# The first expert product by seven half-size products, on one core

## The chip, the cores and the metric

The kernel runs on one core of a Trainium2 chip. The metric is the time of one execution on the device, in microseconds (us); the median of three runs of the kernel before is 1385.63 us (1385.61 to 1385.86).

## The reference

Three stages follow one another on 1536 tokens (2 batches of 768) of width 512.

```
# 1: attention, 8 heads of 64; a key is kept if it is a sink (pos < n_sink) or 0 <= rel < window
a = softmax(where(keep, scale * q @ k.T, -1e9));  x = a @ v          # x: 1536 x 512
# 2: h = x @ w_in (512 x 1024); s = h * softmax(h); x2 = layernorm(s) * g_ln @ w_out (1024 x 512)
# 3: 8 experts, a gate from the logits of x2
P = exp(x2 @ w_gate - max)
for _ in range(8):
    P /= P.sum(1, keepdims=True) + 1e-09; P /= P.sum(0, keepdims=True) + 1e-09; P *= N / E
for e in range(E):
    out += P[:, e:e + 1] * (np.maximum(x2 @ w1[e], 0.0) @ w2[e])     # w1: 512 x 1024, w2: 1024 x 512
```

## The kernel before

All matrices are fp32. A product is made of three fast ones: each operand is split into a rounded part `hi` and a rest `lo`, and `mm3` adds hi x hi, hi x lo and lo x hi in PSUM. Such a step is therefore three matmul instructions (lines 80, 82 and 84). The rest comes from a subtraction: on VectorE for what leaves PSUM (`split_psum`: ScalarE copies, VectorE subtracts), on GpSimd for weights, which lie in SBUF (`split_sbuf`: a copy at line 73, subtractions of 512 columns at line 77).

Stages 1 and 2 go through 12 blocks of 128 tokens, one head at a time, in numbered slots. `h_unit` makes h for one block and starts its chain of softmax and LayerNorm steps: maximum (line 243), exponential on ScalarE, product, square on ScalarE, some small operations on `st` of which one is on GpSimd (line 260), scale and shift (line 264), the gains on GpSimd (line 265), and transposes on TensorE back to `lt`. `x2_unit` then multiplies two blocks with w_out in matmuls of 256 tokens; its PSUM tile `x2p` has one buffer, and `split_psum` takes it to `x2T`, with the tokens as columns.

Stage 3 is `experts`. For each expert e and each of 3 groups g of 512 tokens it computes the first product in 8 blocks of 128 of f, each with 4 blocks `kk` of d (12 matmuls of 512 columns), a relu on ScalarE and its rest on VectorE (tile `ht`), and then the second product for 4 blocks of tokens, 8 blocks of f each (24 matmuls of 512 columns). Results are added to `acc` on VectorE with the gate as a factor (line 690). Weights come in pieces of 512 KB; `pump` splits the next one when a piece has been used. The gate's logits and its iterations (`sinkhorn`) are cut into steps that `step_side` puts between the experts' matmuls.

Two things set the order. The program is written in slots, and `beside` gives attention work a higher priority than the matmuls that `bulk` takes from a queue. A scheduler then puts the instructions of each engine in a row, by priorities and by when it thinks that operands are ready; in that way matmuls of a later step come ahead where an earlier one waits. Pools that are opened and closed (`att`, `wp`, the PSUM pools) give their memory to what comes next, and what takes it waits for the last reader.

Of the kernel before, what the change touches and what calls it, by code (L numbers as in the profile page):

```python
# [21 lines left out]
def tile_sink_attention__then__solu_moe__then__sinkhorn_moe(  # L22
# [29 lines left out]
    W = 2 * C  # L52
    scale = 1.0 / float(D) ** 0.5
    PS = bass.MemoryType.PSUM

    def f32(ap):
        return ap.bitcast(F32)
# [33 lines left out]
    gains = const.tile([P, F], F32, name="gains")  # L91
# [43 lines left out]
    wraw = wpool = None  # L135
    w_extra = []
    w_tiles = [None] * 16
    w_count = [0]

    def w_slot():  # L140
        n = w_count[0] % (8 + len(w_extra))
        w_count[0] += 1
        tp, nm = (w_extra[n], f"we{n}") if n < len(w_extra) else (wpool, f"w{n - len(w_extra)}")
        return tp.tile([P, 2, F], F32R, name=nm, tag=nm)

    def w_split(src):
        raw = wraw.tile([P, F], F32, name="wr", tag="wr")
        nc.sync.dma_start(out=raw.rearrange("p (a b) -> p a b", b=src.shape[-1]), in_=src)
        t = w_slot()
        split_sbuf(t[:, 0], t[:, 1], raw)  # L150
        return t
# [75 lines left out]
    def h_unit(t, xt, pp, later, tr_q):  # L227
# [35 lines left out]
        def s_ln():  # L263
            nc.vector.tensor_scalar(u, u, nmu, c, ALU.add, ALU.mult)
            nc.gpsimd.tensor_tensor(u, u, gains, ALU.mult)
# [26 lines left out]
    x2T = {}  # L292

    def x2_unit(p, pp):

        lt = ln.pop(p)
        dst = x2T[p // 2]
        cs = slice((p % 2) * 2 * P, (p % 2 + 1) * 2 * P)
        for d2 in range(KD // 2):
# [9 lines left out]
            split_psum(dst[:, 0, ds, cs], dst[:, 1, ds, cs], ps)  # L309
# [238 lines left out]
    def logits_units(lp, ps_pool, lg):  # L548
# [7 lines left out]
        for g in range(NG):  # L556
            ps = ps_pool.tile([32, 512], F32, name="lgp", tag="mm")
            for kk in range(KD):
                nc.tensor.matmul(ps, lhsT=wg_r[:, kk], rhs=x2T[g][:, 0, kk], start=(kk == 0), stop=False)
            for kk in range(KD):  # L560
                nc.tensor.matmul(
                    ps[0:E], lhsT=wg_r[:, kk, 0:E], rhs=x2T[g][:, 1, kk], start=False, stop=(kk == KD - 1)
                )
            nc.scalar.activation(out=lt[:, g * 512:(g + 1) * 512], in_=ps[0:16], func=ACTF.Copy)
        yield
# [7 lines left out]
    def sinkhorn(lp, ps_pool, pr):  # L573

        lg = lp.tile([P, T, E], F32, name="lg")
        yield from logits_units(lp, ps_pool, lg)
# [34 lines left out]
    def experts(hpool, opool, lp, ps_pool):  # L611
        pr = lp.tile([P, T, E], F32, name="pr")
        acc = [opool.tile([P, DM], F32, name=f"acc{t}") for t in range(T)]
        side = sinkhorn(lp, ps_pool, pr)
        gate_done = [False]
        raw_blocks = []

        def step_side():
            if gate_done[0]:
                return  # L620
            try:
                next(side)
            except StopIteration:
                gate_done[0] = True
                for t in raw_blocks:
                    nc.gpsimd.tensor_scalar(acc[t], acc[t], pr[:, t, 0:1], 0.0, ALU.mult, ALU.add)

        w_list = []
        for e in range(E):
            for c in range(4):  # L630
                w_list.append(w1[e, :, c * 256:(c + 1) * 256].rearrange("(a p) f -> p a f", p=P))
            for c in range(4):
                w_list.append(w2[e, c * 256:(c + 1) * 256, :].rearrange("(a p) d -> p a d", p=P))
        NW = 8 + len(w_extra)
        got = {}
        done = [0]
        asked = [0]

        def pump():
            while asked[0] < len(w_list) and asked[0] < done[0] + NW:  # L640
                got[asked[0]] = w_split(w_list[asked[0]])
                asked[0] += 1

        pump()
        for e in range(E):
            for g in range(NG):
                hts = []
                for f in range(KF):
                    wt = got[8 * e + f // 2]
                    ps = ps_pool.tile([P, 512], F32, name="p1", tag="mm")  # L650
                    for kk in range(KD):
                        c0 = kk * 256 + f % 2 * P
                        for _ in mm3(
                            ps, wt[:, 0, c0:c0 + P], wt[:, 1, c0:c0 + P], x2T[g][:, 0, kk], x2T[g][:, 1, kk],
                            kk == 0, kk == KD - 1,
                        ):
                            yield 0.217
                    ht = hpool.tile([P, 2, 512], F32R, name="ht", tag="ht")
                    nc.scalar.activation(out=ht[:, 0], in_=ps, func=ACTF.Relu)  # L659
                    nc.vector.scalar_tensor_tensor(  # L660
                        out=ht[:, 1], in0=ps, scalar=0.0, in1=f32(ht[:, 0]), op0=ALU.max, op1=ALU.subtract
                    )
                    hts.append(ht)
                    if g == NG - 1 and f % 2:
                        done[0] += 1
                        pump()
                    if f % 2:
                        step_side()
# [349 lines left out]
```

## Time and profile before

| | |
|---|---|
| median of 3 runs | 1385.63 us |
| profiled execution, its own time | 1384.35 us |
| span of its trace | 1382.6 us |
| busy share of TensorE, VectorE, ScalarE, GpSimd | 98%, 30%, 21%, 25% |
| DMA queue, share of the 16 engines' span | 13.4% |

The span is that of the recorded instructions; the execution's own time is 1.75 us longer. Records of TensorE's matmuls overlap, since they are pipelined; distances between starts give their pace. Attention and x2 take the first 331 us of the span, the experts the rest.

### The profile page before, as it was taken

Reading aid. Unit: us, or ns where it says so; the run is one execution under the profiler, and the core shown is the slowest. Engines: PE = TensorE matmul, PEld = TensorE weight load, DVE = VectorE, ACT = ScalarE, POOL = GpSimd, SP = SyncE. Lnnn points to the kernel's source line nnn. Section 1 sums busy time; section 2 is a strip of 40 time slices with the busy share of each in tenths; the row PEclk is TensorE's granted clock in tenths of the full one; section 3 lists DMA queues with packets and bytes.
Section 4 is the critical chain, followed back from the end, with each engine's and each line's share of the span. In section 5 each row is a group of like instructions: output and inputs, shape, how many; then the busy total and the mean of one; then the engine's idle time right before and its main releaser. Section 6 shows DMA issues by size and latency. Waiting matters only on the chain.

```text
span 1382.6 us, 15901 instructions
## 1 busy us (share of the span) xinstructions
PE 1354.8 (98%) x6599; PEld 1125.9 (81%) x6599; DVE 411.9 (30%) x860; ACT 296.6 (21%) x628; POOL 348.1 (25%) x360
## 2 busy tenths in 40 slices
PE   7799999999999999999999999999999999999998
PEld 5688888887888888888888888888888888888886
DVE  7976544542233111221112221122211221112211
ACT  5765545522111100111001110011100110011100
POOL 7862111237005400440142025004400440042000
PEclk9979999999999999999999999999999999999999
DMA  7411211013001200110021012001200210010000
GB/s 215 144 39 32 46 32 24 24 38 100 16 1 48 74 0 1 62 61 0 6 65 52 0 31 76 16 1 46 77 0 0 62 61 0 0 62 24 23 31 33
DMA packets 68354, 56.24 MB, mean 41 GB/s; under 512 B 39984, under 2 KB 56368, under 8 KB 68272
## 3 DMA queue, kind: packets, MB, share of 16 engines
q1 hardware_dynamic: 68272, 55.13, 13.4%
q8 instruction: 54, 0.88, 0.3%
q14 instruction: 28, 0.23, 0.1%
HBM read 51.97 MB, written 3.15 MB: 40 GB/s over the span
## 4 chain that ended last, share of the span: by engine, by line
PE 92%; DVE 3%; ACT 1%; issue 0%; POOL 0%
PE p L80 25%; PE p L84 25%; PE p L82 25%; PE av L518 2%; PE x2p L80 2%; PE x2p L82 2%; PE x2p L84 2%; PE hp L84 1%; PE hp L80 1%; PE hp L82 1%; PE trp L490 1%; PE trp L320 1%; PE sc L80 1%; PE trp L276 1%; PE sc L82 1%; PE sc L84 0%
## 5 line engine op out<-in xcount | busy, mean ns | idle before, releaser
L659 ACT ACTIVATE ht<-p 128x512 fp32r<-128x512 f32 x192 | 114.8, 598 | 844.2 <-PE p L84 844.2
L80 PE MATMUL p<-x2T,w 128*128 128x512 f32 x672 | 262.0, 390 | 0.0
L82 PE MATMUL p<-x2T,w 128*128 128x512 f32 x672 | 261.5, 389 | 0.0
L84 PE MATMUL p<-x2T,w 128*128 128x512 f32 x672 | 261.5, 389 | 0.0
L80 PE MATMUL p<-w,ht 128*128 128x512 f32 x672 | 259.4, 390 | 0.0
L82 PE MATMUL p<-w,ht 128*128 128x512 f32 x672 | 258.9, 389 | 0.0
L84 PE MATMUL p<-w,ht 128*128 128x512 f32 x672 | 258.9, 389 | 0.0
L660 DVE SCALAR_TENSOR_TENSOR ht<-p,ht 128x512 fp32r<-128x512 f32 x192 | 132.7, 691 | 414.9 <-ACT ht L659 414.9
L73 POOL TENSOR_SCALAR w<-wr 128x1024 fp32r<-128x1024 f32 x56 | 59.1, 1056 | 610.3 <-PE p L84 601.9
L690 DVE SCALAR_TENSOR_TENSOR acc<-p,pr,acc 128x512 f32<-128x512 f32 x84 | 63.1, 751 | 382.4 <-PE p L84 382.4
L80 PEld LDWEIGHTS p<-x2T,w 128*128 128x128 f32 x672 | 126.2, 188 | 26.3
L84 PEld LDWEIGHTS p<-w,ht 128*128 128x128 f32 x672 | 126.2, 188 | 26.2
L84 PEld LDWEIGHTS p<-x2T,w 128*128 128x128 f32 x672 | 126.2, 188 | 26.2
L82 PEld LDWEIGHTS p<-x2T,w 128*128 128x128 f32 x672 | 126.2, 188 | 26.0
L80 PEld LDWEIGHTS p<-w,ht 128*128 128x128 f32 x672 | 126.2, 188 | 26.0
L82 PEld LDWEIGHTS p<-w,ht 128*128 128x128 f32 x672 | 126.2, 188 | 26.0
L77 POOL TENSOR_TENSOR w<-wr,w 128x512 fp32r<-128x512 f32 x112 | 142.1, 1290 | 4.3
L80 PE MATMUL x2p<-lt,w 128*128 128x256 f32 x192 | 56.1, 292 | 0.2
L82 PE MATMUL x2p<-lt,w 128*128 128x256 f32 x192 | 55.8, 290 | 0.0
L84 PE MATMUL x2p<-lt,w 128*128 128x256 f32 x192 | 54.6, 284 | 0.0
L518 PE MATMUL av<-v,at 128*128 128x64 f32 x352 | 52.8, 295 | 0.6 <-ACT at L493 0.5
L518 PEld LDWEIGHTS av<-v,at 128*128 128x128 f32 x352 | 49.9, 215 | 3.6 <-ACT at L493 1.4
(173 smaller groups left out, 1506.9 us busy)
## 6 DMA issues: line engine op xcount, KB each, us to landing
wr<-in_moe_w_dram SPq DMA_DIRECT2D x64, 512.0 KB, 3.3
raw<-in_moe_w_in_dram SPq DMA_DIRECT2D x8, 512.0 KB, 5.7
raw<-in_moe_w_out_dram SPq DMA_DIRECT2D x8, 512.0 KB, 3.6
qk<-in_q_dram SPq DMA_DIRECT2D x12, 256.0 KB, 2.8
qk<-in_k_dram SPq DMA_DIRECT2D x12, 256.0 KB, 2.9
v<-in_v_dram SPq DMA_DIRECT2D x12, 256.0 KB, 2.8
out_dram<-acc SPq DMA_DIRECT2D x12, 256.0 KB, 2.0
gains<-in_moe_g_ln_dram SPq DMA_DIRECT2D x1, 512.0 KB, 5.4
```

The source lines that it names most:

```text
L73: nc.gpsimd.tensor_scalar(hi, src, 1.0, 0.0, ALU.mult, ALU.add)
L77: nc.gpsimd.tensor_tensor(lo[:, cs], src[:, cs], f32(hi[:, cs]), ALU.subtract)
L80: nc.tensor.matmul(ps, lhsT=lh, rhs=rh, start=start, stop=False)
L82: nc.tensor.matmul(ps, lhsT=lh, rhs=rl, start=False, stop=False)
L84: nc.tensor.matmul(ps, lhsT=ll, rhs=rh, start=False, stop=stop)
L276: nc.tensor.transpose(ps[:, j], u[:, f * P:(f + 1) * P], ident)
L320: nc.tensor.transpose(ps[:, j], src[:, 2 * j:2 * j + 2].rearrange("p h d -> p (h d)"), ident)
L490: nc.tensor.transpose(ps[:, hh, z], a[:, o:o + P], ident)
L518: nc.tensor.matmul(self.av_ps[:, h], lhsT=at[:, hh, z], rhs=self.raw["v", tv][:, h], start=h == 0 and n == 0, stop=h == H - 1 and n == len ...
L659: nc.scalar.activation(out=ht[:, 0], in_=ps, func=ACTF.Relu)
L660: nc.vector.scalar_tensor_tensor(out=ht[:, 1], in0=ps, scalar=0.0, in1=f32(ht[:, 0]), op0=ALU.max, op1=ALU.subtract)
L690: nc.vector.scalar_tensor_tensor(out=acc[t], in0=ps, scalar=pr[:, t, e:e + 1], in1=acc[t], op0=ALU.mult, op1=ALU.add)
```

## The change

The first product is done by Strassen's scheme in the variant with 15 sums (Winograd's). The half sizes are of f (1024 to 2 x 512), of d (512 to 2 x 256) and of the tokens (a half n has 768, as two blocks of 384). One unit is a slice s (128 of f in each of the two halves of f, 32 slices for the 8 experts) with one token half n. `first` makes its four result blocks with seven products of 2 x 3 matmuls of 384 columns, where the plain way takes eight. The sums of weights (S1 to S4) are made on GpSimd in `split_w1`, those of x2 (T1 to T4) once for each half in `build_x`, on VectorE and GpSimd, before they are split into hi and lo. The sums of products are made in PSUM: three banks `pb`, `pd` and `pz` receive a copy or a sum from ScalarE or VectorE, and later products add to it. `seed` writes `pb` and `pd` once with matmuls ahead of that.

`second` then takes 2 x 128 of f for six blocks of 128 tokens: 6 matmuls of 512 columns each, and one addition to `acc` for each, four times as many as before. The gate is ready at slice 3, so what has been added until then is multiplied by it there. `run` puts the second product of one unit between the steps of the first of the next. `x2_unit` now copies its result as fp32 to `x2f` (four of the six pairs whole on ScalarE, two half on ScalarE and half on VectorE), and `build_x` splits it later.

The diff below is cut to its core; the removed loops of `experts` stand in the listing above.

```diff
-        dst = x2T[p // 2]
-        cs = slice((p % 2) * 2 * P, (p % 2 + 1) * 2 * P)
+        for b in {2 * p // 3, (2 * p + 1) // 3} - set(x2f):
+            x2f[b] = xa_tile(b, [P, KD, NX])
...
-            split_psum(dst[:, 0, ds, cs], dst[:, 1, ds, cs], ps)
+            t = 2 * p
+            if t % 3 < 2:
+                c = t % 3 * P
+                nc.scalar.activation(out=x2f[t // 3][:, ds, c:c + 2 * P], in_=ps, func=ACTF.Copy)
+            else:
+                nc.scalar.activation(out=x2f[t // 3][:, ds, 2 * P:], in_=ps[:, :, 0:P], func=ACTF.Copy)
+                nc.vector.tensor_copy(x2f[t // 3 + 1][:, ds, 0:P], ps[:, :, P:])
...
+        def build_x(self, n, tp):
+            x = self.x[n] = self.xp[n].tile([P, 7, 2, 2, NX], F32R, name=f"x{n}")
+            b11, b21 = x2f[2 * n][:, 0:2], x2f[2 * n][:, 2:4]
+            b12, b22 = x2f[2 * n + 1][:, 0:2], x2f[2 * n + 1][:, 2:4]
+            def put(k, src):
+                nc.scalar.activation(out=x[:, k, 0], in_=src, func=ACTF.Copy)
+                nc.vector.tensor_tensor(out=x[:, k, 1], in0=src, in1=f32(x[:, k, 0]), op=ALU.subtract)
+            def minus(e, z, a, b):
+                t = tp(z)
+                e.tensor_tensor(out=t, in0=a, in1=b, op=ALU.subtract)
+                return t
+            t3 = minus(nc.gpsimd, 0, b22, b12)
+            t1 = minus(nc.vector, 1, b12, b11)
+            put(self.X11, b11)
+            put(self.T3, t3)
+            put(self.X21, b21)
+            t2 = minus(nc.vector, 0, b22, t1)
+            put(self.T1, t1)
+            t4 = minus(nc.gpsimd, 1, b21, t2)
+            put(self.T2, t2)
+            put(self.T4, t4)
+            put(self.X22, b22)
...
+        def split_w1(self, s):
+            r = self.raw.pop(("1", s))
+            w = self.w1[s] = self.w1p[s % 2].tile([P, 2, 7, 2, P], F32R, name=f"w1_{s % 2}", tag="w1")
+            g = nc.gpsimd
+            g.tensor_tensor(r[:, 4], r[:, 0], r[:, 3], ALU.add)
+            g.tensor_tensor(r[:, 6], r[:, 1], r[:, 0], ALU.subtract)
+            g.tensor_tensor(r[:, 5], r[:, 4], r[:, 1], ALU.subtract)
+            g.tensor_tensor(r[:, 7], r[:, 2], r[:, 5], ALU.subtract)
+            src = r[:, 1:8].rearrange("p k a b -> p (k a b)")
+            hi, lo = (w[:, z].rearrange("p k a b -> p (k a b)") for z in range(2))
+            split_sbuf(hi, lo, src)
...
+        def seed(self):
+            x = self.x[0][:, 0, 0, 0]
+            for tag in "bd":
+                nc.tensor.matmul(self.bank(tag), lhsT=x[:, 0:P], rhs=x, start=True, stop=True)
+        def product(self, ps, w, k, x, kx, start):
+            for kk in range(2):
+                wh, wl = w[:, 0, k, kk], w[:, 1, k, kk]
+                xh, xl = x[:, kx, 0, kk], x[:, kx, 1, kk]
+                for z, (a, b) in enumerate(((wh, xh), (wh, xl), (wl, xh))):
+                    nc.tensor.matmul(
+                        ps, lhsT=a, rhs=b, start=start and kk == 0 and z == 0, stop=kk == 1 and z == 2,
+                        skip_group_check=True,
+                    )
...
+        def first(self, s, n):
+            w, x = self.w1[s], self.x[n]
+            A11, A12, A22, S1, S2, S3, S4 = range(7)
+            h = [self.hp.tile([P, 2, 2, NX], F32R, name=f"h{j}", tag=f"h{j}", bufs=2) for j in range(2)]
...
+            def relu(j, f, ps):
+                nc.scalar.activation(out=h[j][:, f, 0], in_=ps, func=ACTF.Relu)
+                nc.vector.scalar_tensor_tensor(
+                    out=h[j][:, f, 1], in0=ps, scalar=0.0, in1=f32(h[j][:, f, 0]), op0=ALU.max, op1=ALU.subtract
+                )
+            pz = self.bank("z")
+            self.product(pz, w, S3, x, self.T3, True)
+            z = self.hp.tile([P, NX], F32, name="z", tag="z", bufs=2)
+            nc.scalar.activation(out=z, in_=pz, func=ACTF.Copy)
+            yield
+            pa = self.bank("a")
+            self.product(pa, w, A11, x, self.X11, True)
+            pb = self.bank("b")
+            nc.scalar.activation(out=pb, in_=pa, func=ACTF.Copy)
+            yield
+            self.product(pa, w, A12, x, self.X21, False)
+            self.product(pb, w, S2, x, self.T2, False)
+            relu(0, 0, pa)
+            pd = self.bank("d")
+            nc.vector.tensor_tensor(out=pd, in0=pb, in1=z, op=ALU.add)
+            yield
+            self.product(pb, w, S1, x, self.T1, False)
+            nc.vector.tensor_tensor(out=pz, in0=pb, in1=z, op=ALU.add)
+            yield
+            self.product(pd, w, A22, x, self.T4, False)
+            self.product(pb, w, S4, x, self.X22, False)
+            relu(0, 1, pd)
+            relu(1, 1, pz)
+            relu(1, 0, pb)
+            self.h = h
+        def second(self, s, n, h):
+            e, i = divmod(s, NI)
+            w = self.w2[s]
+            for j in range(2):
+                for tb in range(3):
+                    b = 2 * n + j
+                    t = 3 * b + tb
+                    if (s, tb) == (0, 0):
+                        self.acc[b] = xa_tile(b, [P, 3, DM])
+                    acc = self.acc[b][:, tb]
+                    ps = self.bank("2", 3, [P, DM])
+                    for f in range(2):
+                        hs = h[j][:, f, :, tb * P:(tb + 1) * P]
+                        for _ in mm3(ps, hs[:, 0], hs[:, 1], w[:, 0, f], w[:, 1, f], f == 0, f == 1):
+                            pass
+                    if s == 0:
+                        nc.scalar.activation(out=acc, in_=ps, func=ACTF.Copy)
+                    elif s < NI - 1:
+                        nc.vector.tensor_tensor(out=acc, in0=ps, in1=acc, op=ALU.add)
+                    else:
+                        if s == NI - 1:
+                            assert self.gate_done
+                            nc.gpsimd.tensor_scalar(acc, acc, self.pr[:, t, 0:1], 0.0, ALU.mult, ALU.add)
+                        nc.vector.scalar_tensor_tensor(
+                            out=acc, in0=ps, scalar=self.pr[:, t, e:e + 1], in1=acc, op0=ALU.mult, op1=ALU.add
+                        )
+                    if s == E * NI - 1:
+                        nc.sync.dma_start(out=out[t * P:(t + 1) * P, :], in_=acc)
+                    yield
...
+            units = []
+            for s in range(0, NS, 2):
+                if s < NI:
+                    units += [(s, 0), (s + 1, 0), (s, 1), (s + 1, 1)]
+                else:
+                    units += [(s, 0), (s, 1), (s + 1, 0), (s + 1, 1)]
+            last = {s: u for u, (s, n) in enumerate(units)}
+            self.seed()
+            before = None
+            for u, (s, n) in enumerate(units):
+                if u == 1:
+                    self.build_x(1, lambda z: self.temp(("tt", "h1")[z]))
+                if u < 2:
+                    step_side()
+                    step_side()
+                a = self.first(s, n)
+                b = self.second(*before, self.h) if before else iter(())
+                for _ in range(6):
+                    next(a, None)
+                    if u > 1:
+                        step_side()
+                    next(b, None)
+                if before and last[before[0]] == u - 1:
+                    self.refill("2", before[0] + 2)
+                if last[s] == u:
+                    self.refill("1", s + 2)
+                before = (s, n)
+            for _ in self.second(*before, self.h):
...
+        def begin(self):
+            self.build_x(0, lambda z: self.temp(("tt", "wr")[z]))
+            self.load_w1(0)
+            self.split_w1(0)
+            self.load_w1(1)
+            self.load_w2(0)
+        def go_on(self):
+            for s in range(2):
+                self.split_w2(s)
+                self.load_w2(s + 1)
+            self.split_w1(1)
+            self.load_w1(2)
+            self.run()
...
-                x2T[NG - 1] = pool(stack, "x2b", side="right").tile([P, 2, KD, 512], F32R, name="x2T2")
-                w_extra.append(pool(stack, "we0", side="right"))
-                w_count[0] = 0
-                wraw = pool(stack, "wraw", bufs=2, side="right")
-                hpool = pool(stack, "hp", bufs=8, side="right")
+                ex.open_early(stack)
                 psum_a.close()
-                mmp = pool(stack, "ps_m2", bufs=3, space=PS)
                 queue.append((s, x2_unit(T // 2 - 2, pp)))
                 queue.append((s + 10, x2_unit(T // 2 - 1, pp)))
+        ex.begin()
         att2.close()
-        opool = pool(stack, "op")
-        for _ in experts(hpool, opool, opool, mmp):
-            pass
+        wp.close()
+        psum_b.close()
+        ex.open_rest(stack)
+        ex.go_on()
```

TensorE's row where x2 ends, before: `x2p<-lt` are the last pair's matmuls, `p<-x2T,we` the first expert's, `lgp` the logits'; lines 80, 82 and 84 are the three of `mm3`.

```order
L80 MATMUL x2p<-lt,w_891 128x256
L82 MATMUL x2p<-lt,w_891 128x256
L84 MATMUL x2p<-lt,w_891 128x256
L80 MATMUL p_3429<-x2T_1010,we_3377 128x512
L82 MATMUL p_3429<-x2T_1010,we_3377 128x512
L80 MATMUL p_3445<-x2T_1010,we_3377 128x512
L82 MATMUL p_3445<-x2T_1010,we_3377 128x512
L559 MATMUL lgp<-x2T_1010,wg_r 32x512 x4
L561 MATMUL lgp<-x2T_1010,wg_r 8x512 x4
L80 MATMUL x2p<-lt,w_430 128x256
```

The same place after the change; the x2 matmuls of the last pair (now lines 83, 85, 87) end here, `pb` and `pd` are the seeds, `lgp` the logits, and line 716 is a product of the scheme, six matmuls.

```order
L83 MATMUL x2p<-lt,w_891 128x256
L85 MATMUL x2p<-lt,w_891 128x256
L87 MATMUL x2p<-lt,w_891 128x256
L709 MATMUL pb<-x_3345 128x384
L709 MATMUL pd<-x_3345 128x384
L564 MATMUL lgp<-x_3345,wg_r 32x384 x4
L566 MATMUL lgp<-x_3345,wg_r 8x384 x4
L716 MATMUL pz<-x_3345,w_0_3373 128x384 x6
L716 MATMUL pa<-x_3345,w_0_3373 128x384 x6
```

Before, expert and logits matmuls stood between the x2 matmuls; now all of them stand behind the last, and the logits come with the first unit's products.

TensorE's row in the middle of the experts, after the change: `p_4804` and its like are the second product of the unit before, `pz`, `pa`, `pb` the products of this one, `x` the built operand, `w_1` the split sums of weights.

```order
L716 MATMUL pb<-x_3534,w_0_4403 128x384 x6
L83 MATMUL p_4804<-w_4527,h_4669 128x512
L85 MATMUL p_4804<-w_4527,h_4669 128x512
L83 MATMUL p_4821<-w_4527,h_4669 128x512
L85 MATMUL p_4821<-w_4527,h_4669 128x512
L83 MATMUL p_4845<-w_4527,h_4669 128x512
L85 MATMUL p_4845<-w_4527,h_4669 128x512
L716 MATMUL pz<-x_3345,w_1_4533 128x384 x6
L87 MATMUL p_4804<-w_4527,h_4669 128x512
L87 MATMUL p_4821<-w_4527,h_4669 128x512
L87 MATMUL p_4845<-w_4527,h_4669 128x512
L716 MATMUL pa<-x_3345,w_1_4533 128x384 x6
```

Before, this part of the row was `mm3` steps of one result tile after another, 12 or 24 matmuls each; now second-product matmuls stand between products of the next unit.

VectorE's row while the last block's LayerNorm chain runs, after the change: lines 235 to 256 on `st` and `u` are the chain (before: lines 243 to 264), lines 649 and 645 are `build_x(0)`, which makes `x_3345`, and line 313 takes part of an `x2p` tile.

```order
L235 TENSOR_REDUCE st<-hp 128x1
L649 TENSOR_TENSOR wr<-xa_1973,xa_1503 128x768
L645 TENSOR_TENSOR x_3345<-xa_1503,x_3345 128x768 x2
L645 TENSOR_TENSOR x_3345<-xa_1973,x_3345 128x768
L68 TENSOR_TENSOR lt<-trp,lt 128x4x128 x2
L241 ISA u,st<-hp,u 128x1024
L241 ISA st 128x1
L245 TENSOR_SCALAR st<-st 128x1
L313 COPY xa_3126<-x2p 128x2x128
L645 TENSOR_TENSOR x_3345<-tt,x_3345 128x768
L645 TENSOR_TENSOR x_3345<-wr,x_3345 128x768
L244 TENSOR_SCALAR st<-st 128x1
```

Before, none of the lines 649, 645 and 313 existed; the chain's operations now have them in between.

## Rows read from the trace of the kernel before

**Rows 1.** The page, part 1: busy us, share of the span, instructions.

```profile
PE 1354.8 (98%) x6599; PEld 1125.9 (81%) x6599; DVE 411.9 (30%) x860; ACT 296.6 (21%) x628; POOL 348.1 (25%) x360
```

**Rows 2.** The page, part 4: the chain that ended last, by engine.

```profile
PE 92%; DVE 3%; ACT 1%; issue 0%; POOL 0%
```

**Rows 3.** Windows: stretch, length, busy us of PE, PEld, DVE, ACT, POOL, clock, DMA share, GB/s.

```profile
340.00:1377.00 1037.00, 1036.55 (x4581) 858.14 (x4580) 212.45 (x349) 120.55 (x202) 207.50 (x178) 1.00 0.10 31
```

**Rows 4.** Groups by form on PE: count | busy us, mean ns | idle before.

```profile
L80 PE MATMUL p<-x2T,w 128*128 128x512 f32 x672 | 262.0, 390 | 0.0
...
L80 PE MATMUL p<-we,ht 128*128 128x512 f32 x96 | 37.4, 389 | 0.0
```

**Rows 5.** Timeline of PE, 800.20 to 810.40: start, duration, instruction; 45 matmuls.

```profile
800.20 0.39 PE L84 MATMUL p<-w,ht 128*128 128x512 f32 x1
...
810.40 0.39 PE L84 MATMUL p<-w,ht 128*128 128x512 f32 x1
```

**Rows 6.** Timeline of PE in the last x2 pair; 27 matmuls.

```profile
328.05 0.28 PE L84 MATMUL x2p<-lt,w 128*128 128x256 f32 x1
...
331.25 0.28 PE L84 MATMUL x2p<-lt,w 128*128 128x256 f32 x1
```

**Rows 7.** Durations of one line or tile: lowest/median/highest ns, first and last.

```profile
L659 ACT ACTIVATE ht<-p x192: 597/598/601, 313.5 to 1354.8; 128x512 fp32r<-128x512 f32 x192
...
L660 DVE SCALAR_TENSOR_TENSOR ht<-p,ht x192: 677/691/693, 314.1 to 1355.5; 128x512 fp32r<-128x512 f32 x192
...
L690 DVE SCALAR_TENSOR_TENSOR acc<-p,pr,acc x84: 749/751/753, 490.6 to 1376.6; 128x512 f32<-128x512 f32 x84
...
L73 POOL TENSOR_SCALAR w<-wr x56: 1045/1058/1065, 298.5 to 1245.6; 128x1024 fp32r<-128x1024 f32 x56
...
L77 POOL TENSOR_TENSOR w<-wr,w x112: 1266/1290/1310, 306.5 to 1248.0; 128x512 fp32r<-128x512 f32 x112
...
L261 DVE TENSOR_TENSOR st<-st x12: 148/159/1242, 74.9 to 306.6; 128x1 f32<-128x1 f32 x12
...
L264 DVE TENSOR_SCALAR u<-u,st x12: 800/804/1780, 76.3 to 307.8; 128x1024 f32<-128x1024 f32 x12
...
L80 PEld LDWEIGHTS x2p<-lt,w x192: 186/188/193, 109.2 to 330.9; 128*128 128x128 f32 x192
```

**Rows 8.** The page, part 6: DMA issues, KB each, us from issue to landing.

```profile
wr<-in_moe_w_dram SPq DMA_DIRECT2D x64, 512.0 KB, 3.3
```

**Rows 9.** Timeline of PE around the last x2 pair.

```profile
302.44 0.40 PE L80 MATMUL p<-x2T,we 128*128 128x512 f32 x1
...
315.57 1.03 PE L276 MATMUL trp<-ident,u 128*128 128x128 f32 x8
...
318.30 0.28 PE L80 MATMUL x2p<-lt,w 128*128 128x256 f32 x1
```

**Rows 10.** Timeline of DVE and POOL there: start, duration; in brackets idle before, releaser.

```profile
299.39 1.23 DVE L243 TENSOR_REDUCE st<-hp 128x1 f32<-128x1024 f32 x1 [7.08 <-PE hp L84]
...
306.56 1.24 DVE L261 TENSOR_TENSOR st<-st 128x1 f32<-128x1 f32 x1 [0.67 <-POOL st L260]
307.84 1.75 DVE L264 TENSOR_SCALAR u<-u,st 128x1024 f32<-128x1024 f32 x1
...
306.49 2.55 POOL L77 TENSOR_TENSOR w<-wr,w 128x512 fp32r<-128x512 f32 x2
...
309.67 2.41 POOL L265 TENSOR_TENSOR u<-u,gains 128x1024 f32<-128x1024 f32 x1 [0.63 <-DVE u L264]
```

**Rows 11.** Timeline of PE at a stall, and windows after it, as in rows 3.

```profile
61.33 0.38 PE L80 MATMUL sc<-kh,qT 64*128 64x264 f32 x1 [2.14 <-DVE a L453]
...
64.00:66.00 2.00, 2.00 (x11) 1.78 (x10) 2.00 (x7) 0.21 (x1) 1.63 (x2) 0.50 0.03 8
...
72.00:74.00 2.00, 2.00 (x8) 1.59 (x7) 1.97 (x6) 2.00 (x6) 1.61 (x3) 0.79 0.57 131
```

**Rows 12.** Timeline of DVE at the end of the span.

```profile
1376.59 0.75 DVE L690 SCALAR_TENSOR_TENSOR acc<-p,pr,acc 128x512 f32<-128x512 f32 x1 [4.69 <-PE p L84]
```

More of the change, by code (lines that the diff above doesn't have):

```diff
@@ L555, in logits_units @@
         lt = lp.tile([16, NT], F32, name="lt16")
[L556 to L557 removed]
+        for b in range(4):
+            parts = x_parts(b)
+            ps = ps_pool.tile([32, NX], F32, name="lgp", tag="mm")
             for kk in range(KD):
[L559 removed]
+                nc.tensor.matmul(ps, lhsT=wg_r[:, kk], rhs=parts[kk // 2][:, 0, kk % 2], start=(kk == 0), stop=False)
             for kk in range(KD):
                 nc.tensor.matmul(
[L562 removed]
+                    ps[0:E], lhsT=wg_r[:, kk, 0:E], rhs=parts[kk // 2][:, 1, kk % 2], start=False, stop=(kk == KD - 1)
                 )
[L564 to L565 removed]
+            nc.scalar.activation(out=lt[:, b * NX:(b + 1) * NX], in_=ps[0:16], func=ACTF.Copy)
+            yield
         ps = ps_pool.tile([P, T, 16], F32, name="lgt", tag="mm")
@@ L707, in fast_path @@
     def fast_path(stack):
-        nonlocal wraw, wpool
-        wpool = pool(stack, "wp")
-        pool(stack, "edge", side="right").tile([P, 248], F32, name="edge")
-        att, att2, early, psum_a = (ExitStack() for _ in range(4))
+        nonlocal wpool
+        pool(stack, "edge", side="right").tile([P, 24], F32, name="edge")
+        wp, att, att2, early, psum_a, psum_b = (ExitStack() for _ in range(6))
+        wpool = pool(wp, "wp")
         a2 = pool(att2, "att2")
@@ L733, in fast_path @@
         fast.load_sinks(0)
+        pp["gains"] = gains = a2.tile([P, F], F32, name="gains")
         nc.sync.dma_start(out=gains, in_=g_ln.rearrange("(o f) -> o f", o=1).to_broadcast([P, F]))
@@ L797, in fast_path @@
                     early.close()
-                    xp = pool(stack, "x2a", side="right")
-                    for g in range(NG - 1):
-                        x2T[g] = xp.tile([P, 2, KD, 512], F32R, name=f"x2T{g}")
+                    xa.append(pool(stack, "xa", side="right"))
             with beside():
@@ L883, in general_path @@
                 split_w_out(n, ep)
-        xp = pool(stack, "gx2", side="right")
-        for g in range(NG):
-            x2T[g] = xp.tile([P, 2, KD, 512], F32R, name=f"gx2T{g}")
+        xa.append(pool(stack, "gxa", side="right"))
         with ExitStack() as att:
@@ L890, in general_path @@
             pp = {"st": a2, "u": a2, "lnT": a2, "mhalf": mhalf}
+            pp["gains"] = a2.tile([P, F], F32, name="ggains")
+            nc.sync.dma_start(out=pp["gains"], in_=g_ln.rearrange("(o f) -> o f", o=1).to_broadcast([P, F]))
             for nm, bufs in (("h", 2), ("tr", 2), ("mm", 2)):
@@ L967, in general_path @@
                         pass
-        wraw = pool(stack, "gwraw", bufs=2)
-        hpool = pool(stack, "ghp", bufs=8)
-        opool = pool(stack, "gop")
-        mmp = pool(stack, "gps_m2", bufs=8, space=PS)
-        for _ in experts(hpool, opool, opool, mmp):
-            pass
+        wp.close()
+        ex = Experts()
+        ex.open_early(stack)
+        ex.begin()
+        ex.open_rest(stack)
+        ex.go_on()
     with ExitStack():
```

195 lines of the change are left out of this document (92 added, 103 removed).

## The prediction, made before the change was run

> **What bounds the kernel now.** I read the page from the top: busy shares, chain, then the trace by stage. TensorE is busy for 98% of the span and carries 92% of the chain that ended last [rows 1, 2]. The stage table says where: from 340 us to 1377 us TensorE is busy for 1036.55 of 1037 us at full clock, while VectorE, ScalarE and GpSimd have 212, 121 and 208 us of work there [rows 3]. So the expert stage is a matmul stream and nothing else; its length is the number of matmuls times their pitch, and one microsecond of stream removed is one microsecond of time, until another engine makes TensorE wait.
>
> The form table gives six groups of 672 and six of 96: 4608 matmuls of 512 columns, half of them `p<-x2T` (first product), half `p<-w,ht` (second) [rows 4]. Their durations (390 ns) overlap, so the pitch is taken from start times: 45 matmuls between 800.20 and 810.40, 0.2267 us each [rows 5]. 4608 x 0.2267 = 1044.6 us, which is the stage.
>
> **The change, part by part.** *First product.* It had 8 experts x 3 token groups x 8 blocks of f x 4 blocks of d x 3 = 2304 matmuls of 512 columns: 522.3 us. Now a unit (one slice of f, one half of the tokens) has 7 products x 2 x 3 = 42 matmuls of 384 columns, and there are 32 x 2 = 64 units: 2688 matmuls. No 384-column matmul stands in the trace. The x2 stage has 256-column ones, back to back at full clock: 27 between 328.05 and 331.25, 0.1185 us each [rows 6]. The bounds are therefore 0.1185 and 0.2267; these two points lie close to a line (0.42 ns a column and some 10 ns fixed), and 384 is their middle: 0.1726 us. 2688 x 0.1726 = 463.9 us, a gain of **58.4**. The second product keeps 36 x 64 = 2304 matmuls of 512 columns. A unit costs 42 x 0.1726 + 36 x 0.2267 = 15.4 us.
>
> *What must hide under a unit.* ScalarE: six copies or relus of 384; at the whole price of the 512 form, 0.60 us, that is 3.6 us. VectorE: four residuals (0.69), two sums from PSUM into PSUM (no row; bounded by 0.69 and twice that) and six additions to acc (0.75): 8.7 to 10 us. GpSimd per slice, two units or 30.8 us: 2816 elements copied (1.06 us per 1024) and 3840 added or subtracted (1.29 per 512): 12.6 us [rows 7]. Transfers per slice: 512 KB of w2 as now, 3.3 us [rows 8], and four of 128 KB with shorter runs, between 3.3 and 13 us together. All fit; if cover were gone the largest, VectorE's, would still be below 15.4.
>
> *The new waits in a unit.* Products accumulate onto sums that ScalarE and VectorE write, so TensorE waits for round trips. The order shows that the scheduler puts second-product matmuls between. The tightest is S4 -> relu -> residual -> copy of pa into pb -> A12. From the start of S4's last matmul: its record 0.39, then 0.60 + 0.69 + 0.60 at 512 prices, and four hand-overs of some 0.05: 2.5 us. Ahead of A12 stand 0.17 + six second-product matmuls (1.36) + S3 (1.04) + three more (0.68) = 3.25 us. It holds even with the copy into PSUM at double price (3.1). Behind the relu on ScalarE wait only this copy and that of z, so nothing else gets late. The sums (pd, pz) have over 2 us of slack each. I cost the loop's waits at nothing.
>
> *The hand-over to the experts is where it pays.* Three things are late there.
>
> (a) Before, 24 first-product matmuls and 18 of 24 logits matmuls (counted in the order) ran ahead of the last x2 matmul (331.25), in the time in which TensorE waits for the last token block's LayerNorm; one such block starts at 302.44 [rows 9]. Now the order puts every expert matmul behind it: +5.4 us (24 x 0.2267). Of the logits, 32 of 384 columns and two seeds stand behind it instead of 6: 34 x 0.1726 - 6 x 0.2267 = +4.5 us.
>
> (b) The LayerNorm chain of the last block gets longer. It starts with the maximum at 299.39 and the pair of x2 that needs it starts at 318.30, 18.9 us later [rows 9, 10]. Now the first operand build stands inside that chain: three ScalarE copies of 768 columns (0.90 each by 598 ns per 512 [rows 7]) ahead of the exponential, since `x0` takes memory that `xt` held until the last h matmul, and nine VectorE operations of 768 (1.03 each by 691 ns per 512) among the chain's own. Counting along both queues I get the product with the gains some 5.5 us later. Sixteen x2 matmuls more stand ahead of the last h matmul (+1.9). Against that, the transposes no longer wait for first-product and logits matmuls: before, the gains ended at 312.08 and TensorE came to them at 315.57; about 4.4 us come back. Sum +3.
>
> How much longer depends on GpSimd. A VectorE addition of one column, 0.16 us elsewhere, took 1.24 at 306.56 and ended as the first of two 1.28 us splits on GpSimd (from 306.49) did; the next operation took 1.75 in place of 0.80 [rows 7, 10]. Residuals that read PSUM do not show it: 192 between 677 and 693 ns [rows 7]. So operations that read and write SBUF alone wait for GpSimd's, and the build has nine beside 4.5 us of weight splits. That adds 0 to 5 us: +3 to +8, I take +5.2. The x2 bank is now freed by one copy instead of copy and residual: -0.7.
>
> The Trainium skill, "SBUF — State Buffer", section "Who interferes with whom", says the same as a rule: a VectorE instruction with two SBUF inputs and a GpSimd one that reads SBUF exclude each other, and whoever starts second waits in full. The row at 306.56 agrees. By that rule the upper end, +8, would stand in the sum, and part (c) would be 12 us.
>
> And the clock: after 2.14 us in which TensorE had nothing, the granted clock fell to 0.50 (1.2 GHz) and was on its way back some 10 us after the stall at 61 us (0.50 from 64 us, 0.79 from 72 to 74) [rows 11]. TensorE will now wait twice for several microseconds, for the evacuation of `x2p` that stands behind the build on VectorE's queue, and for the transposes. Ten microseconds at half rate cost 5; part falls into a wait anyway: +2.5. Together (b) moves the end of x2 from 331.5 to some 338.5: **+7**.
>
> (c) Behind it the first units wait: no second product lies between the products of the first one, `w2`'s and `w1`'s splits must follow the last x2 matmul (their memory held w_out), about 20 us of GpSimd work, and the second build has eleven SBUF-only VectorE operations beside them. Without blocking I count 3 us of TensorE waits, with it 9, and a further clock fall up to 5: I take **+7**.
>
> Small terms: the multiplication of twelve acc blocks by the gate at slice 3 (+1), the last unit's second product alone at the end (+1); before, 6 us passed between the last addition's start and the end of the span [rows 3, 12], and this stays.
>
> *Sum:* -58.4 + 5.4 + 4.5 + 7 + 7 + 2 = **-32.5 us**. The profiled execution took 1384.35 us with a span of 1382.6, so 1351.9 for the like; the median, 1385.63, lies 1.3 above it: **1353 us**.
>
> **Rivals.** *The hand-over is almost free:* only (a) is paid, with 2 us of waits: -58.4 + 9.9 + 2 = -46.5, 1339 us. For it: GpSimd's splits may be done before the build begins; against it: the order of VectorE's queue. *Weight loads set the pace (slower):* each matmul has its own load, and a load's record lasts 188 ns [rows 7], longer than 173. If loads could not overlap each other, a product's pitch would be 0.188: 2688 x 0.0154 = +41.4, 1394.5 us; it decides from a pitch of 0.185 on, where 522.3 - 26 us of other costs are used up. Against it: at 256 columns the same loads stand 0.1185 apart and their records overlap. *The loop waits:* a round trip exceeds its cover, say by 0.5 us a unit: 64 x 0.5 = +32, 1385 us, no change. For it: sums and copies from PSUM to PSUM have no row; against: 0.75 us of slack at high prices. *The clock falls in the loop or again and again at the start:* 15 us more, 1368. That the change does nothing can be excluded: the order has its 2688 and 2304 matmuls.
>
> **How the numbers follow.** My forecast 0.70, free hand-over 0.10, loop waits 0.08, loads 0.06, clock 0.06. The forecast's own bounds: hand-over (b) from +2 to +12 and (c) from +3 to +14 give 1344 to 1365. Taking in the free hand-over, the range is 1338 to 1367; loop waits, loads and the clock case (0.20) are left out. A measurement of this kernel tells about 0.2% (2.8 us) from no change. Faster: 0.87 (forecast, free hand-over, clock, a little of the loop case); within 0.2%: 0.03; slower: 0.10.
>
> **What would show it.** Pitch of 384-column matmuls 0.172 to 0.174 us and a unit of 15.4 us in mid-stream, TensorE without idle there; between 300 and 325 us two TensorE waits and a granted clock of 0.50; x2 ending near 338; stream ending near 1344. Wrong would be a pitch of 0.185 or more, a unit above 15.7, idle before A12 in every unit, or a stream that starts as early as before.

## The result and the profile after

The changed kernel takes 1362.2 us (median of 4 runs, 1360.61 to 1362.86) against 1385.63: a ratio of 0.9829, 95% interval 0.9812 to 0.9846, 23.4 us less where 32.5 were forecast (1353; range 1338 to 1367). The profiled execution took 1362.57 us with a span of 1360.5; the forecast for that span was 1350.1.

Page, parts 1 and 4, against [rows 1, 2]:

```profile
PE 1317.5 (97%) x6993; PEld 1171.5 (86%) x6993; DVE 708.2 (52%) x1352; ACT 373.4 (27%) x837; POOL 541.9 (40%) x560
...
PE 89%; DVE 4%; ACT 1%; issue 1%; POOL 0%; DVEq 0%; POOLq 0%; ACTq 0%
```

TensorE is still the bound. Windows (columns as in rows 3; the last but two is the granted clock) show where it is not busy or not at full clock:

```profile
310.00:320.00 10.00, 8.54 (x48) 8.34 (x48) 8.83 (x15) 2.82 (x5) 4.99 (x5) 0.64 0.10 29
...
312.00:317.00 5.00, 5.00 (x25) 5.00 (x25) 4.26 (x8) 2.80 (x4) 2.68 (x2) 0.50 0.00 0
...
350.00:360.00 10.00, 9.16 (x41) 8.11 (x42) 6.78 (x10) 3.19 (x6) 9.92 (x8) 0.83 0.27 68
...
700.00:1000.00 300.00, 300.00 (x1498) 271.25 (x1497) 143.48 (x230) 53.79 (x114) 119.73 (x115) 1.00 0.12 35
```

The hand-over on TensorE's timeline, against [rows 9]:

```profile
311.42 0.58 PE L83 MATMUL x2p<-lt,w 128*128 128x256 f32 x1 [8.86 <-DVE xa L313]
311.80 0.41 PE L85 MATMUL x2p<-lt,w 128*128 128x256 f32 x1
...
317.13 0.34 PE L87 MATMUL x2p<-lt,w 128*128 128x256 f32 x1
...
322.43 1.09 PE L268 MATMUL trp<-ident,u 128*128 128x128 f32 x8 [2.47 <-POOL u L257]
...
338.03 0.28 PE L87 MATMUL x2p<-lt,w 128*128 128x256 f32 x1
...
339.90 1.20 PE L716 MATMUL pz<-x,w 128*128 128x384 f32 x6
...
350.84 0.50 PE L87 MATMUL p<-w,h 128*128 128x512 f32 x1 [2.12 <-DVE h L729]
```

TensorE waits 8.86 us for VectorE's copy of `x2p` and 2.47 us for the gains; x2 ends at 338.15 (forecast 338.5). Between 311.80 and 317.13 the 256-column matmuls stand 0.213 us apart instead of 0.1185 [rows 6]: the granted clock fell while TensorE had no work, and is 0.50 here, its lower level (1.2 GHz). VectorE and GpSimd at the time (timelines):

```profile
303.28 5.35 DVE L645 TENSOR_TENSOR x<-xa,x 128x768 fp32r<-128x768 f32 x3
...
310.96 0.41 DVE L313 COPY xa<-x2p 128x256 f32<-128x256 f32 x1
311.29 0.94 DVE L645 TENSOR_TENSOR x<-tt,x 128x768 fp32r<-128x768 f32 x1
...
301.25 6.56 POOL L80 TENSOR_TENSOR w<-wf,w 128x512 fp32r<-128x512 f32 x4
```

Three of the build's subtractions take 5.35 us (1.78 each) while GpSimd splits weights (301.25 to 307.81), one takes 0.94 after it: the wait of [rows 10] again, and the copy that TensorE needs stands behind them.

One unit in mid-stream:

```profile
802.19 1.23 PE L716 MATMUL pz<-x,w 128*128 128x384 f32 x6
803.25 0.86 PE L87 MATMUL p<-w,h 128*128 128x512 f32 x3
803.95 1.23 PE L716 MATMUL pa<-x,w 128*128 128x384 f32 x6
805.02 1.22 PE L716 MATMUL pb<-x,w 128*128 128x384 f32 x6
806.07 0.39 PE L83 MATMUL p<-w,h 128*128 128x512 f32 x1
...
810.20 1.04 PE L716 MATMUL pa<-x,w 128*128 128x384 f32 x5
...
817.87 1.21 PE L716 MATMUL pz<-x,w 128*128 128x384 f32 x6
```

Nothing is marked idle, yet this unit takes 15.68 us; from the tenth unit (489.29) to the last (1334.15) they take 15.646 on average where 15.41 was forecast. 64 x 0.235 = 15 us: that is the open question. A record of a 512-column matmul lasts 0.39 us and the next starts 0.23 us later, so up to 0.16 us of waiting leaves no idle in such rows; only start times show it. Taken one by one from the tenth unit on, they show none here: behind the start of a 384-column matmul the next comes at most 0.185 us later, behind a 512-column one at most 0.236, the same largest distances as in the streams of experiment 1, which have nothing to wait for.

### The profile page after: what moved, and what is told of

Same layout as the page of the kernel before. It is cut to its first block, busy times and chain, and to the rows that moved or that the text cites. A ratio compares the mean times of both kernels' runs of the same rounds, so it can differ in the third digit from the quotient of the medians.

```text
span 1360.5 us, 17867 instructions
## 1 busy us (share of the span) xinstructions
PE 1317.5 (97%) x6993; PEld 1171.5 (86%) x6993; DVE 708.2 (52%) x1352; ACT 373.4 (27%) x837; POOL 541.9 (40%) x560
## 4 chain that ended last, share of the span: by engine, by line
PE 89%; DVE 4%; ACT 1%; issue 1%; POOL 0%; DVEq 0%; POOLq 0%; ACTq 0%
PE pb L716 15%; PE p L87 13%; PE p L85 13%; PE p L83 13%; PE pa L716 10%; PE pd L716 5%; PE pz L716 5%; PE av L522 2%; PE x2p L83 2%; PE x2p L85 2%; PE x2p L87 1%; PE hp L87 1%; PE hp L83 1%; PE hp L85 1%; DVE x L645 1%; PE trp L494 1%
## 5 line engine op out<-in xcount | busy, mean ns | idle before, releaser
L783 DVE SCALAR_TENSOR_TENSOR xa<-p,pr,xa 128x512 f32<-128x512 f32 x348 | 250.7, 748 | 207.0 <-PE p L87 207.0
L85 PE MATMUL p<-w,h 128*128 128x512 f32 x768 | 301.3, 392 | 0.0
L83 PE MATMUL p<-w,h 128*128 128x512 f32 x768 | 300.1, 391 | 0.5 <-DVE xa L783 0.5
L87 PE MATMUL p<-w,h 128*128 128x512 f32 x768 | 282.0, 394 | 2.1 <-DVE h L729 2.1
L716 PE MATMUL pb<-x,w 128*128 128x384 f32 x1152 | 234.0, 338 | 0.0
L716 PEld LDWEIGHTS pb<-x,w 128*128 128x128 f32 x1152 | 206.0, 188 | 5.7
L87 PEld LDWEIGHTS p<-w,h 128*128 128x128 f32 x768 | 143.6, 188 | 28.7 <-DVE h L729 2.5
L716 PE MATMUL pa<-x,w 128*128 128x384 f32 x768 | 167.1, 340 | 0.2 <-DVE h L729 0.2
L83 PEld LDWEIGHTS p<-w,h 128*128 128x128 f32 x768 | 144.2, 188 | 25.4 <-issue 0.9
L85 PEld LDWEIGHTS p<-w,h 128*128 128x128 f32 x768 | 144.2, 188 | 21.5
L716 PEld LDWEIGHTS pa<-x,w 128*128 128x128 f32 x768 | 139.2, 189 | 13.8 <-DVE h L729 0.5
L80 POOL TENSOR_TENSOR w<-wf,w 128x512 fp32r<-128x512 f32 (+1 forms) x128 | 148.3, 1191 | 2.6
L716 PE MATMUL pz<-x,w 128*128 128x384 f32 x384 | 78.0, 338 | 0.0
L83 PE MATMUL x2p<-lt,w 128*128 128x256 f32 x192 | 58.1, 303 | 10.1 <-DVE xa L313 8.9
```

The source lines that it names most:

```text
L80: nc.gpsimd.tensor_tensor(lo[:, cs], src[:, cs], f32(hi[:, cs]), ALU.subtract)
L83: nc.tensor.matmul(ps, lhsT=lh, rhs=rh, start=start, stop=False)
L85: nc.tensor.matmul(ps, lhsT=lh, rhs=rl, start=False, stop=False)
L87: nc.tensor.matmul(ps, lhsT=ll, rhs=rh, start=False, stop=stop)
L716: nc.tensor.matmul(ps, lhsT=a, rhs=b, start=start and kk == 0 and z == 0, stop=kk == 1 and z == 2, skip_group_check=True,)
L783: nc.vector.scalar_tensor_tensor(out=acc, in0=ps, scalar=self.pr[:, t, e:e + 1], in1=acc, op0=ALU.mult, op1=ALU.add)
```

## Experiments

Spans of single executions are not compared below 3 us: x2 ends between 337.7 and 341.3 us in executions whose program is the same up to there. Units are compared by start times.

**1. The streams by themselves.** The first two streams' code:

```diff
-            for u, (s, n) in enumerate(units):
+            for u, (s, n) in enumerate(units[:8]):
...
+            for k in range(N):
+                ps = tiles[k % 3][:, 0:NX]
+                for i, (a, b) in enumerate(ops(k)):
+                    nc.tensor.matmul(ps, lhsT=a, rhs=b, start=i == 0, stop=i == 5, skip_group_check=True)
+            for k in range(N):
+                ps = tiles[k % 3]
+                for i, (a, b) in enumerate(ops(k, True)):
...
```

> After eight units of the changed kernel the expert loop is left out, and TensorE runs ten streams one behind another instead, each of 21 times 6 matmuls: 384 columns alone; 512 alone; the two in turn; 384 with small reads by ScalarE (waits, little traffic); 384 with whole copies out of PSUM; 384 with ScalarE writing the PSUM bank in place; 512 with VectorE's additions to acc; 384 beside GpSimd's subtractions; 384 beside VectorE's SBUF subtractions. In the loop of the changed kernel a unit took 15.645 us where 15.41 was forecast: some 0.1766 us for 384 columns and 0.2285 for 512. Theory A (the size's own price): 384 alone shows 0.176, 512 alone 0.2267. Theory B (changing between sizes and result banks costs): both alone are at 0.1726 and 0.2267, in turn the pair of six and six is above 2.396 us by some 30 ns. Theory C (traffic of the other engines in PSUM or SBUF): only the streams beside another engine's work lie above 0.1726 or 0.2267, by 2 to 4 ns a matmul. Theory D (waits and signals): the stream with small reads is above by as much as the loop.

Each stream's first row (timeline; L873 384 alone, L877 512 alone, L881 and L884 in turn, L888 with small reads, L893 with whole copies):

```profile
478.22 2.10 PE L873 MATMUL p<-x,w 128*128 128x384 f32 x11
...
500.09 1.55 PE L877 MATMUL p<-w,h 128*128 128x512 f32 x6
...
528.68 1.23 PE L881 MATMUL p<-x,w 128*128 128x384 f32 x6
529.75 1.53 PE L884 MATMUL p<-w,h 128*128 128x512 f32 x6
...
579.78 1.40 PE L888 MATMUL p<-x,w 128*128 128x384 f32 x7
...
601.65 6.57 PE L893 MATMUL p<-x,w 128*128 128x384 f32 x37
```

384 alone: 21.87 us for 126, 0.1736 each; 512 alone: 28.59, 0.2269. In turn a pair of six and six takes 51.10 / 21 = 2.433 us, 30 ns more than the two alone (2.403). With small reads: 21.87 again; the others, beside ScalarE's copies out of or in PSUM, VectorE or GpSimd, are at 21.84 to 21.87 (384) and 28.59 (512). The streams of 384 that follow matmuls of 512 take 21.87, those that follow 384 take 21.84: the difference, 30 ns, goes with one change of size to 384. So theory B, as far as these streams go (384 alone is 1 ns above its 0.1726); A, C and D fall.

**2. No weights after slice 3.**

```diff
+            if s >= 4:
+                (self.w1 if which == "1" else self.w2)[s] = (self.w1 if which == "1" else self.w2)[2 + s % 2]
+                return
```

> Weights from slice 4 on are not loaded, summed or split; the loop goes on with those of slices 2 and 3. GpSimd and the DMA queues have nothing to do from about 420 us on. If GpSimd's or the transfers' traffic slows TensorE, a unit falls from 15.645 to some 15.4 us and the span by 13 us, to about 1347; if not, the unit stays within 0.02 us of 15.645 and the span within 2 us of 1360.5.

```profile
PE 1316.8 (97%) x6993; PEld 1170.1 (86%) x6993; DVE 707.4 (52%) x1352; ACT 373.6 (28%) x837; POOL 189.7 (14%) x224
```

GpSimd's work falls from 541.9 to 189.7 us, and a unit stays at 15.646; the span is 1358.4. Neither GpSimd nor the transfers slow the loop.

**3. Eight products in the same slices.**

```diff
-            self.product(pz, w, S3, x, self.T3, True)
...
+            for f in range(2):
+                for j in range(2):
+                    ps = self.bank("abdz"[2 * f + j])
+                    self.product(ps, w, 1 - f, x, (self.X11, self.X12)[j], True, False)
+                    self.product(ps, w, 2 + f, x, (self.X21, self.X22)[j], False, True)
+                    relu(j, f, ps)
+                    yield
```

> Slices of 256 of f and halves of the tokens as in the change, but the first product by the plain eight products in half sizes: no sums of operands, none in PSUM. 48 matmuls of 384 a unit instead of 42. If the pitches of the loop belong to the sizes, a unit is 48 x 0.1766 + 36 x 0.2285 = 16.7 us and 64 units are 1069 us, 68 more than the scheme's 1001; if the sums written into PSUM and their waits slow TensorE, it is 48 x 0.1726 + 36 x 0.2267 = 16.45 us. The hand-over has only two thirds of the build and less splitting, so x2 should end some 2 to 4 us before 338.3.

```profile
330.88 0.28 PE L87 MATMUL x2p<-lt,w 128*128 128x256 f32 x1
...
492.82 2.26 PE L699 MATMUL pz<-x,w 128*128 128x384 f32 x12
...
1395.19 2.25 PE L699 MATMUL pz<-x,w 128*128 128x384 f32 x12
```

1418.3 us in one run. A unit takes (1395.19 - 492.82) / 54 = 16.711 us: as dear a pitch as the scheme's, without one sum in PSUM, and with as many changes of size (ten a unit, counted in both traces). So the scheme itself brings 68 us of stream. Against the kernel before, slices of 256 with 384 columns cost some 33 us in all, 25 of them in the stream (64 x 16.711 against 1044.6). x2 ends at 331.0: four operands without sums cost the hand-over little or nothing, the seven operands with their sums 7 us.

**4. The build held until the gains.** One VectorE operation reads `u` and writes into `x0` ahead of the build.

```diff
+            if after is not None:
+                nc.vector.tensor_scalar(x[:, :, 0, 0, 0:1], after[:, 0:7].rearrange("p (a b) -> p a b", b=1), 1.0, 0.0, ALU.mult, ALU.add)
```

> The first operand build is made to wait for the last block's LayerNorm product with the gains, by one small VectorE operation that reads it and writes into the build's tile ahead of it. If the build inside the chain is what moved x2's end from 331.5 to 338.3, the chain from maximum to transposes takes some 13 to 15 us instead of 21.3, the stall for the x2p copy (8.86 us) shrinks below 4, x2 ends near 330 and the span is 6 to 9 us shorter than 1360.5. Rival: the build then stands between x2 and the first unit, and the first product waits for it: the first product still starts near 340 and the time stays within 2 us.

```profile
315.07 1.09 PE L269 MATMUL trp<-ident,u 128*128 128x128 f32 x8 [1.24 <-POOL u L258]
...
319.63 0.58 PE L83 MATMUL x2p<-lt,w 128*128 128x256 f32 x1 [3.47 <-ACT lt L67]
...
323.75 0.58 PE L85 MATMUL x2p<-lt,w 128*128 128x256 f32 x1 [3.54 <-DVE lt L68]
```

1362.1 us, ratio to the kernel before 0.9831 (0.9815 to 0.9848): nothing gained. The chain is 7 us shorter (transposes at 315.07, not 322.43), but their evacuation on ScalarE and VectorE now stands behind the build, TensorE waits there twice 3.5 us, and x2 ends at 338.0. A wait had moved, to a place that neither theory named.

**5. Fewer changes of size.** From the ninth unit the order is fixed in groups.

```diff
+                self.order_on = u >= 8
...
-                for _ in range(6):
+                for _ in range(2):
...
+            if self.order_on and self.prev is not None:
+                tc.add_manual_dep(ins.ins, self.prev.name, mybir.DependencyInfo(mybir.DependencyClass.NoSync, mybir.DependencyReason.DATA), reason="order")
```

> From the ninth unit on TensorE's matmuls of the two products are fixed in groups: S3 and A11, 18 of the second product, S2 A12 S1 A22 S4, 18 of the second product; 4 changes between 384 and 512 columns a unit instead of 9.8, the same matmuls and sums. In the first experiment the pair of six and six took 2.433 us in turn against 2.403 from the streams alone, 15 ns a change. If a change of size costs that here, the unit falls from 15.645 to 15.56 us and the span by some 5 us (56 units x 0.088). If only the round trips between engines count, the grouped order has less cover for the sums in PSUM (1.05 us for a sum of 0.57) and a unit gets longer, by up to 0.5 us each, 28 us in all.

```profile
807.49 1.23 PE L722 MATMUL pb<-x,w 128*128 128x384 f32 x6
...
812.78 4.28 PE L778 MATMUL p<-w,h 128*128 128x512 f32 x18
816.91 0.86 PE L722 MATMUL pz<-x,w 128*128 128x384 f32 x4
```

1362.9 us (ratio 0.9834, 0.9818 to 0.9851), with x2 ending 3 us later in the profiled execution. A unit takes 15.606 us, 0.040 less: half of the 0.088 expected. The five products take 5.29 us here (5.21 alone) and the 18 of the second 4.13 (4.08). Short waits for the sums are not the reason: only two distances between starts in 54 units are more than 20 ns above the size's own pitch. A unit has 0.147 us more than its sizes alone, and 0.106 of that lies on the first nine matmuls behind each change of size, 2.9 ns each; in the change it is 0.175 of 0.187, 3.0 ns each. Longer runs have more of these matmuls for each change (36 a unit with four changes, 58 with ten), so six changes less save less than six times the price of one.

**6. More changes of size.** Three and three in turn, order fixed in the same way.

```diff
+                self.order_on = u >= 8
...
-                for _ in range(6):
+                for z in range(15):
                     next(a, None)
```

> The opposite: from the ninth unit on three matmuls of 384 and three of 512 stand in turn, 24 changes a unit. By 15 ns a change a unit is 15.645 + 14.2 x 0.0152 = 15.86 us and the span 12 us longer than 1360.5. If changes cost nothing and the 15.645 comes from elsewhere, the unit stays within 0.03 us of 15.645.

```profile
815.59 0.85 PE L777 MATMUL p<-w,h 128*128 128x512 f32 x3
816.28 0.69 PE L722 MATMUL pb<-x,w 128*128 128x384 f32 x3
816.81 0.85 PE L777 MATMUL p<-w,h 128*128 128x512 f32 x3
817.63 0.80 PE L722 MATMUL pb<-x,w 128*128 128x384 f32 x3
818.26 0.86 PE L777 MATMUL p<-w,h 128*128 128x512 f32 x3
```

1387.2 us in one run; a unit takes 16.094, twice what was expected. The rows show part of it: 0.82 and 0.63 us from start to start for threes that otherwise take 0.69 and 0.53, and at 811.76 there is another such place (0.73 and 0.63). Together that is some 0.37 us a unit in which TensorE waited without an idle mark, so the unit's length does not price a change. Without these four places a unit has 0.26 us more than its sizes alone, 11 ns for each of the 24 changes.

**7. The build held until the last transposes are out.** As in 4, but the small operation reads `lt`.

```diff
+                src = f32(lt[:, 1, KF - 1, 1, 0:7]).rearrange("p (a b) -> p a b", b=1)
+                nc.vector.tensor_scalar(x[:, :, 0, 0, 0:1], src, 1.0, 0.0, ALU.mult, ALU.add)
```

> The first operand build waits for the transposed LayerNorm product of the last block (the small VectorE operation now reads its last evacuated tile), so that the chain and the evacuation of the transposes are free of it. Held back until the product with the gains alone, the build made the evacuation of the transposes wait and x2 ended at 337.9 all the same. Now the transposes should start near 315 us, the x2 matmuls behind them at 317 to 318 instead of 323.8, x2 should end near 331 and the first product start at 333 or when the build is done (12 us of VectorE work from 317: near 330), so the span falls by 5 to 7 us. Rival: the build or the splits of weights end later than x2, the first product starts near 339 as before, and the span stays within 2 us.

```profile
315.77 1.29 PE L269 MATMUL trp<-ident,u 128*128 128x128 f32 x8 [2.21 <-POOL u L257]
317.11 0.58 PE L83 MATMUL x2p<-lt,w 128*128 128x256 f32 x1
...
332.51 0.28 PE L87 MATMUL x2p<-lt,w 128*128 128x256 f32 x1
...
334.38 1.23 PE L720 MATMUL pz<-x,w 128*128 128x384 f32 x6
```

1355.5 us (ratio 0.9783, 0.9766 to 0.9799): 6.7 us faster than the change, with the same units (15.646). The first product starts 5.5 us sooner. So the build inside the chain was most of what the change cost at the hand-over.

**8. Experiments 5 and 7 together.**

> The later build and the grouped order together. If the two terms are separate, the gains add: some 5 us by the grouping and 5 to 7 by the build, a span of 1349 to 1351 and a time near 1351. If the start of the loop only moves its waits, the sum is that of the grouping alone, near 1355.

1352.8 us (1352.14 to 1356.42; ratio 0.9771, 0.9755 to 0.9787), the fastest of all; units 15.609. The interval overlaps that of 7, so the grouping's share in the whole time is not settled.

**9. What of a change costs.** Left-out loop as in 1, eight streams of 24 pairs, order fixed.

> Again the loop is left out after eight units; TensorE runs eight streams of 24 pairs in a fixed order: 384 alone; 384 and 512 of the same operands (x, split sums) six by six; the 384 of both kinds of operands (x with sums, h with w2) six by six; 384 and 512 of both kinds six by six; the same three by three; one by one; 384 alone with the result bank changed every three; six by six with ScalarE's copies, VectorE's additions and GpSimd's subtractions together. Known: 0.1736 and 0.2269 alone, 30 ns more a pair in turn. If the size is what costs, the second and fourth stream have 2.433 us a pair, the third 2.083 (12 x 0.1736), the seventh 0.1736 a matmul. If the operands' place costs, the third shows 2.11. If the result bank costs, the seventh shows 0.178 or more. Three by three should cost 60 ns more than the streams alone, one by one 180, if each change costs the same 15 ns; the shredded loop, 0.45 us a unit above the original for 14 more changes, says more: 32 ns. With all engines at work the pair stays at 2.433 if traffic doesn't matter.

The first stream, 384 alone, has waits of up to 3.5 us at its start and is not used. First rows of the others: L883 sizes only, L888 operands only, L893 both, L898 three by three, L907 one by one, L911 result banks, L916 with traffic:

```profile
502.81 1.20 PE L883 MATMUL pa<-x,w 128*128 128x384 f32 x6
...
561.20 1.21 PE L888 MATMUL pa<-x,w 128*128 128x384 f32 x6
...
611.28 1.21 PE L893 MATMUL pa<-x,w 128*128 128x384 f32 x6
...
669.68 0.69 PE L898 MATMUL pa<-x,w 128*128 128x384 f32 x3
...
728.24 0.34 PE L907 MATMUL pa<-x,w 128*128 128x384 f32 x1
...
785.86 0.34 PE L911 MATMUL pa<-x,w 128*128 128x384 f32 x1
...
810.83 1.20 PE L916 MATMUL pa<-x,w 128*128 128x384 f32 x6
```

Per pair (difference / 24): sizes only 2.433, operands only 2.087 (2.083 alone), both 2.433, three by three 2.440, one by one 2.401, banks 1.040 (0.1734 a matmul). From 810.83 to the last block of 512 (867.85) is 23 pairs and a block of 384: 2.433 with traffic. It is the size, not operands, banks or traffic. But not a price for each change: four changes cost 37 ns, two cost 30, twelve nothing. By the single starts the extra is spread over the matmuls behind a change: in six by six of both kinds the six of 384 stand 1 to 11 ns above their own pitch, 23 together, those of 512 some 8 together. Why one by one costs nothing is open.

## Why the prediction came out as it did

- **The direction and the mechanism** were right: TensorE's stream sets the time, seven products of 384 shorten it, and from the tenth unit on the loop has no wait that the trace shows, as idle or between starts.
- **The step that was mis-sized is the pitch**, "A unit costs 42 x 0.1726 + 36 x 0.2267 = 15.4 us": 15.646 measured, +15.1 us over 64 units. Of the 0.235 us a unit, 0.05 is the pitch of each size alone (42 x 0.1736 + 36 x 0.2269 = 15.459; so the middle between two sizes was nearly right), and 0.19 comes with ten changes of size (counted in the trace). At the 15 ns a change of six by six they would be 0.15; in the loop, whose runs have 1 to 18 matmuls, they cost 19 ns each, nearly all of it on the first nine matmuls behind a change (experiment 5). That mixing sizes costs was not among the rivals; why a matmul behind a change is slower, no run shows.
- **The hand-over (b)** was right in sum, 338.15 against 338.5; that it is so close is luck, since executions of the same program end x2 between 337.7 and 341.3. The chain took 21.3 us from maximum to transposes, the blocked subtractions are in the rows, and the clock cost 2.4 us between 311.8 and 317.1 and about 1.1 from 324.9 to 327.4, against 2.5 forecast. The exclusion that "SBUF — State Buffer" of the Trainium skill states ("Who interferes with whom") agrees again: 1.78 us beside GpSimd, 0.94 alone. The 12 us that the prediction worked out from it for part (c) did not come, as the next point shows.
- **Part (c) and the small terms** were too high: from x2's end (338.15) to that of the last matmul (1354.3) are 1016.2 us; less 64 units (1001.3) and 34 matmuls of logits and seeds (5.9) that leaves 9.0. Of these 4.5 were there before: 1045.1 us from x2's end to the last addition, less 4584 product matmuls at 0.2267 and 1.4 of logits. So 4.5 us instead of 9. TensorE waits only 2.3 us there, and the clock falls once (0.83 in the mean from 350 to 360 us).
- **Sum:** +15.1 - 4.5 - 0.3 = +10.3; the span is 10.4 us above the forecast. The range held by the room that it gave to (b) and (c); the pitch, which missed, had no room of its own in it.
- **Rivals:** weight loads as the bound fell (pitch 0.1736 with loads of 188 ns). The loop case came closest in effect, 0.235 us a unit where 0.5 was its price, but by another cause than the round trips. The clock case fell as well: 1.00 from 700 to 1000 us. A hand-over that is almost free had to be built: experiment 7 gets 6.7 of the 14 us that lay between the two cases.

## What to carry to other kernels

Price a stream of mixed sizes from start times of the mixture itself, and where records overlap don't take a row without idle for one without waits. A price for one change of size does not carry over: it is 15 ns in runs of six, 19 in the loop of the change, 37 in the longer runs of experiment 5. When a side computation is put among a chain's operations, look at every queue that it enters: holding it back to the wrong point only moved the wait to the next evacuation, and holding it back behind the last one was worth 6.7 us, beside 23.4 of the whole change. A scheme that saves an eighth of the multiplications pays for the smaller pieces that it asks for; running the plain scheme in the same pieces (experiment 3) shows the two apart.

## What was not expected of the hardware

Runs of six matmuls of 384 and 512 columns in turn take 30 ns a pair more than apart, three by three 37 ns, one by one nothing. In the loops of experiments 3, 5 and of the change, the first nine matmuls behind a change of size stand 2.9 to 3.0 ns above their size's own pitch, those further behind 0.6 to 0.9. ScalarE copies 384 columns from PSUM to PSUM in 0.47 us, VectorE adds a PSUM and an SBUF operand into PSUM in 0.57, hardly more than the residual that goes to SBUF:

```profile
L729 DVE SCALAR_TENSOR_TENSOR h<-pb,h 128x384 fp32r<-128x384 f32 x64 | 35.6, 557 | 159.5 <-ACT h L728 159.5
...
L750 DVE TENSOR_TENSOR pz<-pb,z 128x384 f32<-128x384 f32 x64 | 36.3, 566 | 76.6 <-PE pb L716 76.6
```
